# Top-k attention with a highway layer on Trainium2: one highway pass for the last rows of two batches, checks of one operation, and another preparation of the first batch

## Chip, cores and metric

The kernel runs on one core of one Trainium2 chip. The metric is the device time in microseconds (us) of one execution; the time before is the median of three runs.

## The reference

Eight batches of eight heads, 576 rows, head dimension 64. In each row of the scores the 32 largest stay and the others are masked, then softmax and the product with v follow. The heads of one row, put side by side, are the 512 inputs of a highway layer.

```python
scores = scale * np.matmul(q, k.transpose(0, 1, 3, 2))
kth = np.partition(scores, -top_k, axis=-1)[..., -top_k:-top_k + 1]
mask = scores >= kth
scores = np.where(mask, scores, -1000000000.0)
scores = scores - np.max(scores, axis=-1, keepdims=True)
attn = np.exp(scores)
attn = attn / (np.sum(attn, axis=-1, keepdims=True) + 1e-09)
x = np.matmul(attn, v)            # then (B, H, S, D) -> (B * S, H * D)
...
H = np.maximum(x @ w_h, 0.0)
T = 1.0 / (1.0 + np.exp(-(x @ w_t + b_t)))
return (T * H + (1.0 - T) * x).astype(np.float32)
```

## The kernel before

**Tiles.** The 576 rows of a batch are four query tiles of 128 rows (every fourth row of the first 512) and a rest of 64 rows. A `Group` (line 47) is one batch and one query tile, or one batch and its rest. It is cut into pairs: two heads of 128 query rows, or, in the rest, two tiles that each hold two heads of 64 rows. A batch has 4 x 4 + 2 = 18 pairs, the whole kernel `NPR` = 144.

**Steps.** The main loop (lines 662 to 728) runs over pairs, with several pairs in flight. Step n does, in this order of the program: `tree(n)`, the first maximum fold on VectorE (DVE), which reads the scores from PSUM (`ps`) and their evacuated half (`z`) and writes `hi`; in odd steps the further folds on DVE and the four integer operations of `minima` on GpSimd (POOL), which give the minima that belong to the folds' maxima; `mask(n - 4)` on ScalarE (ACT); a piece of a highway pass; `av(n - 5)`, the product with v on TensorE (PE) with ACT's copy to `xs`; `scores(n + 1)` on PE and `evac(n + 1)` on ACT; then the long part of DVE's work, lists of the eight largest values (MAX8 and MATCH_REPLACE8) in `tops` and `rest`, whose end, `m4`, holds the 32nd largest value of a row; and `trans(n - 4)`, PE transposes with the exponential on ACT. `Pinned` (line 25) keeps the operations of all engines but SyncE (SP) in the order in which the program gives them; so most lines of the profile are that helper's, L35, and one goes by the names of tiles.

**Highway.** When the last pair of a group has gone through `av`, `norm` (a DVE reciprocal of the row sums and a POOL multiply into `x`) runs at the end of that step, always an even one, and three entries join the list `ffn`, of which each step takes one: `ffn_x` (PE transposes of x into `xtps`, ACT copies `xT` and `xh`), `ffn_h` with `ffn_d` (PE product with w_h, then DVE `d`), and `ffn_t` with `ffn_e` and `ffn_o` (PE product with w_t and ACT tanh, then DVE `d` again, POOL `o`, and the output DMA on SP). The pre part of an entry stands ahead of `av` and `scores` on PE. A rest goes through all of this with 64 rows (`qlen`), eight times in the kernel. `settle` writes three things of each group for a check: `room`, `slack` and `reach`, three POOL operations.

**Loads.** `prep_pair` (line 113) prepares two heads of a batch: `load` (k, q and v, four DMAs each, on SP), `main` for k and for q (four PE transposes into `kqps`, a bank of the pool `fps`, and ACT's copy to `kT` or `qT`), `last` (the 64 rest rows), and `values` (v to bf16 on ACT). `fps` has one bank, in which all `kqps`, `xtps`, `hps` and `tps` take turns; `ztps` has two, for the transposes of `trans`, which begin in step 4. For batch 0 the four pairs of heads are prepared in steps -1 to 2, just ahead of the scores that need them; q of the first pair is loaded on ACT's queue. For other batches this is spread over the steps of the batch before.

**Ends.** `load_weights` (three POOL DMAs) is called in step 1. After the loop the check reduces `room`, `slack` and `reach`, and a flag says whether an exact second version of the whole kernel has to run (line 749); with these inputs it does not run.

Of the kernel before, what the change touches and what calls it, by code (L numbers as in the profile page):

```python
# [16 lines left out]
STEEP = 2.0**100  # L17
TINY = 1.0e-20
WIDE = 600.0
# [27 lines left out]
class Group:  # L47


    def __init__(self, b, qt, gi, H, P):  # L50
        self.b, self.qt, self.gi = b, qt, gi
        self.rem = qt == J
        self.qlen = P // 2 if self.rem else P
        tiles = (
            [(2 * hp, 2 * hp + 1) for hp in range(H // 2)]
            if self.rem
            else [(h,) for h in range(H)]
        )
        self.nt = len(tiles)
        self.pairs = [tiles[i : i + 2] for i in range(0, self.nt, 2)]  # L60


class Ops:
# [31 lines left out]
    def load_pair(self, src, hp, name, eng=None):  # L95
        nc, D, S, R, P = self.nc, self.D, self.S, self.R, self.P
        JP = J * P
        t = self.ldpool.tile([P, J + 1, 2, D], FP32, tag=name, name=name)
        eng = eng or nc.sync
        for hh in range(2):  # L100
            h = 2 * hp + hh
            eng.dma_start(
                t[:, 0:J, hh, :], src(h, 0, JP).rearrange("(p j) d -> p j d", j=J)
            )
            eng.dma_start(t[0:R, J, hh, :], src(h, JP, S))
        return t
# [6 lines left out]
    def prep_pair(self, srcs, hp, prep, qeng=None):  # L113

        nc, D, S, R, P = self.nc, self.D, self.S, self.R, self.P
        JP = J * P
        kT, qT, vb = prep
        ins = {}

        def load():  # L120
            ins["k"] = self.load_pair(srcs[1], hp, "kin")
            ins["q"] = self.load_pair(srcs[0], hp, "qin", qeng)
            ins["v"] = self.load_pair(srcs[2], hp, "vin")

        def main(name, dst):
            kqps = self.fps.tile([P, 512], FP32, tag="fp", name="kqps")
            for c in range(J):
                nc.tensor.transpose(
                    kqps[:, c * P : (c + 1) * P],
                    ins[name][:, c, :, :].rearrange("p h d -> p (h d)"),  # L130
                    self.ident[:],
                )
            nc.scalar.copy(dst[:, hp, 0:JP], kqps[:])

        def last():
            kqps = self.fps.tile([P, 512], FP32, tag="fp", name="kqps")
            for i, name in enumerate("kq"):
                nc.tensor.transpose(
                    kqps[:, i * R : (i + 1) * R],
                    ins[name][0:R, J, :, :].rearrange("p h d -> p (h d)"),  # L140
                    self.ident[0:R, 0:R],
                )
            for i, dst in enumerate((kT, qT)):
                nc.scalar.copy(dst[:, hp, JP:S], kqps[:, i * R : (i + 1) * R])

        def values():
            vdst = vb[:, 2 * hp : 2 * hp + 2, :, 0:D].rearrange("p h c d -> p c h d")
            nc.scalar.copy(vdst[:, 0:J], ins["v"][:, 0:J])
            nc.scalar.copy(vdst[0:R, J], ins["v"][0:R, J])

        return [load, lambda: main("k", kT), lambda: main("q", qT), last, values]
# [49 lines left out]
    def folds(self, k, g, pi):  # L201


        vec, P, S, H = self.nc.vector, self.P, self.S, self.H
        H1, H2, H3 = S // 2, S // 4, S // 8
        if pi == 0:
            g.w2 = self.lpool.tile([P, H, H2 + 24], FP32, tag="w2", name="w2")
        hi, hh, h3 = self.quads[k]
        vec.tensor_tensor(hh[:], hi[:, :, 0:H2], hi[:, :, H2:H1], ALU.max)
        a, b = hh[:, :, 0:H3], hh[:, :, H3:H2]  # L210
        vec.tensor_tensor(h3[:], a, b, ALU.max)
        return vec.tensor_tensor(
            g.w2[:, 2 * pi : 2 * pi + 4, H3:H2], a, b, ALU.min
        )
# [22 lines left out]
    def tops(self, g, t, h3, hl):  # L237


        nc, P, S = self.nc, self.P, self.S  # L240
        H2, H3 = S // 4, S // 8
        vec = nc.vector
        m1, m2, w2 = g.m1[:, t, :], g.m2[:, t, :], g.w2[:, t, :]
        vec.max(m1, h3)
        yield
        w1 = self.wpool.tile([P, H3], FP32, tag="w1", name="w1")
        vec.match_replace(w1[:], m1, h3, NEG)
        yield
        vec.max(m2, w1[:])
        yield  # L250
        vec.match_replace(w2[:, 0:H3], m2, w1[:], NEG)
        yield
        vec.max(w2[:, H2 : H2 + 8], hl[:, 0:H3])
        yield
        vec.max(w2[:, H2 + 8 : H2 + 16], hl[:, H3:H2])

    def rest(self, g, t, lo):


        nc, P, S = self.nc, self.P, self.S  # L260
        H2 = S // 4
        W = H2 + 24
        vec = nc.vector
        w2 = g.w2[:, t, :]
        vec.max(w2[:, H2 + 16 : W], lo)
        yield
        m3 = self.wpool.tile([P, 8], FP32, tag="m3", name="m3")
        vec.max(m3[:], w2)
        yield
        w3 = self.wpool.tile([P, W], FP32, tag="w3", name="w3")  # L270
        vec.match_replace(w3[:], m3[:], w2, NEG)
        yield
        vec.max(g.m4[:, t, :], w3[:])
# [20 lines left out]
    def lists(self, n, g, pi):  # L294
        P, H = self.P, self.H
        if pi == 0:
            for name in ("m1", "m4") if self.exact else ("m1", "m2", "m4"):
                setattr(g, name, self.lpool.tile([P, H, 8], FP32, tag=name, name=name))
# [19 lines left out]
    def settle(self, g):  # L318
# [7 lines left out]
            self.room[:, g.gi, 0:nt, 0:3],  # L326
            thr.unsqueeze(2).to_broadcast([P, nt, 3]),
# [3 lines left out]
        gp.tensor_tensor(  # L331
            self.slack[:, g.gi, 0:nt, 0], g.m2[:, 0:nt, 7], thr, ALU.subtract
        )
        gp.tensor_copy(self.reach[:, g.gi, 0:nt], g.m1[:, 0:nt, 0])
# [70 lines left out]
    def av(self, n, g, pi, vb):  # L405
# [4 lines left out]
        if pi == 0:  # L410
            g.xs = self.xpool.tile([P, self.H * DE], FP32, tag="xs", name="xs")
        ql = g.qlen
        c0 = col = 0 if g.rem else 2 * P
        h0 = g.pairs[pi][0][0]
        for ti, heads in enumerate(g.pairs[pi]):
            for hi, h in enumerate(heads):
                q0 = hi * (P // 2)
                for c in range(J + 1):
                    nc.tensor.matmul(
                        zr[0:ql, col : col + DE],  # L420
# [6 lines left out]
        nc.scalar.copy(g.xs[0:ql, h0 * DE : h0 * DE + col - c0], zr[0:ql, c0:col])  # L427
# [3 lines left out]
    def norm(self, g):  # L431
        nc, P, H, D = self.nc, self.P, self.H, self.D
        ql = g.qlen
        xs3 = g.xs[0:ql, :].rearrange("p (h e) -> p h e", e=D + 1)
        rinv = self.xpool.tile([P, H], FP32, tag="rinv", name="rinv")
# [9 lines left out]
    def ffn_x(self, g):  # L445
        nc, P, n_g, ql = self.nc, self.P, self.n_g, g.qlen
# [16 lines left out]
    def ffn_h(self, g):  # L463
        nc, P, n_g, ql = self.nc, self.P, self.n_g, g.qlen
# [10 lines left out]
    def ffn_d(self, g):  # L475

        ql = g.qlen
# [10 lines left out]
    def ffn_t(self, g):  # L488

        nc, P, n_g, ql = self.nc, self.P, self.n_g, g.qlen  # L490
# [14 lines left out]
    def ffn_e(self, g):  # L505

        ql = g.qlen
# [9 lines left out]
    def ffn_o(self, g, dst):  # L517
        ql = g.qlen
        o = self.fpool.tile([self.P, self.dm], FP32, tag="o", name="o")
        self.nc.gpsimd.tensor_tensor(o[0:ql, :], g.x[0:ql, :], g.d[0:ql, :], ALU.add)  # L520
        self.nc.sync.dma_start(dst, o[0:ql, :])
# [3 lines left out]
def kernel(  # L525
# [17 lines left out]
    assert D == 64 and R == 64 and H % 4 == 0 and dm == 512  # L543
# [13 lines left out]
    nc.vector.tensor_scalar_mul(nident[:], ident[:], -STEEP)  # L557
# [11 lines left out]
    for i in range(2):  # L569
# [5 lines left out]
    room = const([P, NG, H, 3], FP32, "room")  # L575
    nc.gpsimd.memset(room[:], 1.0)
    slack = const([P, NG, H, 1], FP32, "slack")
    nc.gpsimd.memset(slack[:], 1.0)
    reach = const([P, NG, H], FP32, "reach")
    nc.gpsimd.memset(reach[:], 1.0)  # L580
# [8 lines left out]
        room=room, slack=slack, reach=reach,  # L589
    )  # L590

    with ExitStack() as cm:
# [12 lines left out]
        def srcs(b):  # L605
            return [
                (lambda h, r0, r1, t=t: t[b, h, r0:r1, :]) for t in (q, k, v)
            ]

        def out_rows(g):  # L610
            if not g.rem:
                r0 = g.b * S + g.qt
                return out[r0 : r0 + JP : J, :]
            r0 = g.b * S + JP
            return out[r0 : r0 + R, :]

        groups = [
            Group(b, qt, b * nck + qt, H, P) for b in range(B) for qt in range(nck)
# [8 lines left out]
        def prep(b, hp, qeng=None):  # L627
            if hp == 0:
                preps[b] = ops.prep_alloc(vbufs[b % 2])
            return ops.prep_pair(srcs(b), hp, preps[b], qeng)  # L630
# [20 lines left out]
        early = [prep(0, hp, nc.scalar if hp == 0 else None) for hp in range(NHP)]  # L651
# [10 lines left out]
        while step < NPR + 6 or ffn:  # L662
            n = step
            if n + 1 < NHP:
                for piece in early[n + 1][1:4]:
                    piece()
                if n + 2 < NHP:
                    early[n + 2][0]()
            if have(n):
                ops.tree(n)  # L670
                if n % 2:
                    ops.minima(n // 2, ops.folds(n // 2, *pairs[n - 1]))
            if n == 1:
# [18 lines left out]
            ended = have(n - 5) and pairs[n - 5][1] == len(pairs[n - 5][0].pairs) - 1  # L692
# [25 lines left out]
            if ended:  # L718
# [6 lines left out]
                        lambda g=g: (ops.ffn_e(g), ops.ffn_o(g, out_rows(g))),  # L725
# [7 lines left out]
        vec.tensor_reduce(ok[:, 0:1], room[:], op=ALU.min, axis=AX.XYZ)  # L733
        vec.tensor_reduce(ok[:, 1:2], slack[:], op=ALU.min, axis=AX.XYZ)
        vec.tensor_reduce(ok[:, 2:3], reach[:], op=ALU.max, axis=AX.XY)
        bad = const([P, 4], FP32, "bad")
        vec.tensor_scalar(bad[:, 0:1], ok[:, 0:1], TINY, None, ALU.is_lt)
        vec.tensor_scalar(bad[:, 1:2], ok[:, 1:2], 0.0, None, ALU.is_lt)
        vec.tensor_scalar(bad[:, 2:3], ok[:, 2:3], WIDE, None, ALU.is_gt)
# [9 lines left out]
    with tc.If(taken > 0):  # L749
        with tc.For_i(0, B, 1) as b:  # L750
            with ExitStack() as cm:
                ops = Ops(cm, tc, shared, exact=True)
                srcs = [
                    (lambda h, r0, r1, t=t: t[bass.ds(b, 1), h, r0:r1, :].rearrange("o s d -> (o s) d"))
# [58 lines left out]
```

## Time and profile before

| | |
|---|---|
| median of three runs | 925.96 us (923.73 to 926.5) |
| the profiled execution | 925.72 us, its span 923.9 us |
| instructions | 20386 |
| output DMAs (`out_dram<-o`) | 32 of 256 KB, 8 of 128 KB |
| loads of k (`kin`) | 64 of 128 KB, 64 of 16 KB, the same for v and, with two of each on ACT's queue, for q |
| TensorE clock granted, mean | 0.944 of full speed |

A span is the time from the first to the last instruction of the program in one profiled execution. In the lines of the profile, `d<-tps,d 64x512` is an operation that writes tile d and reads tps and d, 64 partitions of 512 elements; `xN` is how many there are. In rows of groups, the figures after the first bar are busy us in total and mean ns of one, those after the second the engine's idle time just before them and what ended it. In the timeline the figures are start and length in us, and square brackets hold the idle time before and its releaser. PEld are TensorE's weight loads, SPq the issue of DMAs on SP.

### The profile page before, as it was taken

To read this page: it belongs to the slowest core of one execution; us is meant where nothing else is said; L and a number is where in the kernel's file an instruction comes from. 1 tells how busy PE (TensorE), PEld (TensorE's weight loads), DVE (VectorE), ACT (ScalarE), POOL (GpSimd) and SP (SyncE) were. 2 spreads that over 40 slices of the span, in tenths; PEclk is the share of its full clock that TensorE was granted. 3 is DMA by queue.
4 is the path that set the end of the run, shared out by engine and by line. 5 is a ranking of instruction groups with operands and counts; after the bars stand their busy time and mean duration, and the time that the engine had idled before them with its cause. 6 is when DMAs were issued, how large, how long until landed. Compare 5 with 4: busy or idle time off the path is not lost.

```text
span 923.9 us, 20386 instructions
## 1 busy us (share of the span) xinstructions
PE 730.8 (79%) x6601; PEld 510.6 (55%) x6601; DVE 873.4 (95%) x4234; ACT 699.2 (76%) x1321; POOL 709.5 (77%) x509
## 2 busy tenths in 40 slices
PE   5687878878788887878888787887879878877774
PEld 3355556555565555555655555655646555555552
DVE  4699999999999999999999999999999999999991
ACT  3488778887787886887878886888868878776772
POOL 3777778877877888777788887887787778877761
PEclk9999899999999998998999999999989989998997
DMA  5731220221103220122202212023100300000000
GB/s 114 138 70 40 51 51 13 58 69 45 38 18 69 61 52 12 46 51 51 51 13 56 50 41 51 13 67 73 46 24 25 71 12 13 12 13 7 13 24 21
DMA packets 123298, 40.33 MB, mean 44 GB/s; under 512 B 117424, under 2 KB 118576, under 8 KB 123184
## 3 DMA queue, kind: packets, MB, share of 16 engines
q1 hardware_dynamic: 120768, 37.48, 16.6%
q0 software_dynamic: 1200, 1.18, 0.8%
q8 instruction: 54, 0.88, 0.4%
q14 instruction: 60, 0.49, 0.2%
q10 hardware_dynamic: 1216, 0.30, 0.1%
HBM read 30.67 MB, written 9.44 MB: 43 GB/s over the span
## 4 chain that ended last, share of the span: by engine, by line
DVE 78%; POOL 8%; PE 7%; ACT 3%; issue 2%; SPq 1%; DMA 1%; POOLq 0%; ACTq 0%; DVEq 0%
DVE w L35 37%; DVE m L35 18%; DVE hi L35 9%; DVE hh L35 6%; DVE d L35 5%; POOL hi L35 4%; DVE h L35 3%; PE ps L35 2%; POOL hh L35 2%; PE zt L35 2%; POOL o L35 1%; PE zr L35 1%; PE xtps L35 1%; POOL x L35 1%; PE kqps L35 1%
## 5 line engine op out<-in xcount | busy, mean ns | idle before, releaser
L35 PE MATMUL ps<-kT,qT 64*128 64x64 f32 (+3 forms) x1280 | 221.9, 473 | 48.8 <-DVE hi L35 47.8
L35 ACT ACTIVATE z<-ps 128x1152 f32<-128x1152 f32 x144 | 163.0, 1132 | 96.7 <-PE ps L35 95.6
L35 POOL TENSOR_TENSOR hh<-hi,hh 128x576 int32<-128x576 int32 x72 | 101.6, 1410 | 171.9 <-DVE w L35 171.7
L35 PE MATMUL zt<-ident,z 128*128 128x128 f32 x1152 | 225.1, 289 | 0.0
L35 ACT ACTIVATE pen<-z,m 128x576 bf16<-128x576 f32 x288 | 224.1, 779 | 0.2 <-DVE m L35 0.2
L35 PE MATMUL zt<-nident,pen 128*128 128x128 bf16 x1152 | 214.5, 226 | 0.0
L35 DVE MAX8 m<-w 128x8 f32<-128x168 f32 (+1 forms) x864 | 203.6, 283 | 0.0
L35 PEld LDWEIGHTS ps<-kT,qT 64*128 64x128 f32 (+1 forms) x1280 | 112.8, 191 | 148.2 <-issue 88.5
L35 POOL TENSOR_TENSOR hi<-hi,z 128x1152 int32<-128x1152 int32 x72 | 190.1, 2641 | 5.6
L35 POOL TENSOR_TENSOR hi<-z,hi 128x1152 int32<-128x1152 int32 x72 | 189.3, 2629 | 5.6
L35 PEld LDWEIGHTS zt<-ident,z 128*128 128x128 f32 x1152 | 169.8, 147 | 18.4
L35 ACT ACTIVATE et<-zt 128x512 bf16<-128x512 f32 x288 | 161.9, 602 | 15.5 <-PE zt L35 14.1
L35 PEld LDWEIGHTS <-pen 128*128 128x128 bf16 x1440 | 161.0, 112 | 6.3 <-ACT pen L35 6.3
L35 DVE MATCH_REPLACE8 w<-m,w 128x72 f32<-128x72 f32 (+1 forms) x576 | 148.3, 265 | 0.0
L35 DVE TENSOR_TENSOR hi<-ps,z 128x576 f32<-128x576 f32 x144 | 106.3, 738 | 21.6 <-ACT z L35 21.5
L35 DVE MAX8 w<-hi 128x8 f32<-128x288 f32 x288 | 116.5, 445 | 0.0
L35 POOL TENSOR_TENSOR hh<-hh,hi 128x576 int32<-128x576 int32 x72 | 101.4, 1408 | 5.6
L35 PEld LDWEIGHTS <-et 128*128 128x128 bf16 (+1 forms) x1600 | 70.4, 104 | 36.3 <-ACT et L35 13.8
L35 PE MATMUL zr<-v,et 128*128 128x65 bf16 (+1 forms) x1600 | 82.4, 199 | 5.1 <-ACT et L35 4.9
L35 DVE MAX8 w<-hh 128x8 f32<-128x72 f32 x576 | 83.9, 216 | 0.0
L35 PE MATMUL zr<-ident,z 128*128 128x128 f32 x288 | 76.8, 320 | 3.9 <-ACT xs L35 3.9
L35 PE MATMUL xtps<-ident,x 128*128 128x128 f32 (+1 forms) x160 | 28.0, 304 | 60.4 <-POOL x L35 51.1
(64 smaller groups left out, 1102.7 us busy)
## 6 DMA issues: line engine op xcount, KB each, us to landing
kin<-in_k_dram SPq DMA_DIRECT2D x64, 128.0 KB, 2.7
vin<-in_v_dram SPq DMA_DIRECT2D x64, 128.0 KB, 2.6
out_dram<-o SPq DMA_DIRECT2D x32, 256.0 KB, 2.3
qin<-in_q_dram SPq DMA_DIRECT2D x62, 128.0 KB, 2.6
kin<-in_k_dram SPq DMA_DIRECT2D x64, 16.0 KB, 2.5
vin<-in_v_dram SPq DMA_DIRECT2D x64, 16.0 KB, 2.3
out_dram<-o SPq DMA_DIRECT2D x8, 128.0 KB, 2.3
qin<-in_q_dram SPq DMA_DIRECT2D x62, 16.0 KB, 2.4
```

The costliest lines, as they stand in the source:

```text
L35: return self._tc.keep_in_program_order(fn(*args, **kw))
```

## The change

- A rest of an even batch has no highway pass of its own. Its heads' results are put into partitions 0 to 63 of a tile `xs` (tag `xr`), those of the next batch's rest into partitions 64 to 127, and one pass of 128 rows follows after the second; its output goes out in two DMAs of 64 rows.
- `settle` is one POOL operation: the second list of maxima `m2` is written into `w2`, which grows by 8 columns, so that `room` has four columns; `slack` and `reach` go. The check looks at three columns' minimum, the fourth's maximum, and the smallest of `scales`, a constant tile that takes the place of `rinv`.
- In the preparation of batch 0, k and q are transposed into the two banks of `ztps` and the rest rows into that of `fps`; q is copied on DVE. The pieces stand after `tree(n)` instead of ahead of it. The first loads of pair 0 (k and q) are split by head over SP's and ACT's queues.
- In all batches the rest rows of a pair of heads come in one DMA, and v in one DMA with longer runs: 8 DMAs a pair instead of 12.
- `nident` is made on ACT instead of DVE, and `load_weights` is called in step 5 instead of 1.

```diff
-    def __init__(self, b, qt, gi, H, P):
+    def __init__(self, b, qt, gi, H, P, joint=False):
         self.b, self.qt, self.gi = b, qt, gi
...
         self.qlen = P // 2 if self.rem else P
+        self.joint = joint and self.rem
+        self.r0 = b % 2 * self.qlen if self.joint else 0
+        self.rows = P if self.joint else self.qlen
         tiles = (
...
-    def load_pair(self, src, hp, name, eng=None):
+    def load_pair(self, src, hp, name, eng=None, other=None):
         nc, D, S, R, P = self.nc, self.D, self.S, self.R, self.P
         JP = J * P
+        eng = eng or nc.sync
+        if name == "vin":
+            t = self.ldpool.tile([P, 2, J + 1, D], FP32, tag=name, name=name)
+            eng.dma_start(
+                t[:, :, 0:J, :].rearrange("p h j d -> p h (j d)"),
+                src(hp, 0, JP).rearrange("h (p j) d -> p h (j d)", j=J),
+            )
+            eng.dma_start(t[0:R, :, J, :], src(hp, JP, S).rearrange("h p d -> p h d"))
+            return t
         t = self.ldpool.tile([P, J + 1, 2, D], FP32, tag=name, name=name)
-        eng = eng or nc.sync
         for hh in range(2):
-            h = 2 * hp + hh
-            eng.dma_start(
-                t[:, 0:J, hh, :], src(h, 0, JP).rearrange("(p j) d -> p j d", j=J)
-            )
-            eng.dma_start(t[0:R, J, hh, :], src(h, JP, S))
+            (other if other and hh else eng).dma_start(
+                t[:, 0:J, hh, :],
+                src(hp, 0, JP)[hh].rearrange("(p j) d -> p j d", j=J),
+            )
+        rest = lambda: eng.dma_start(
+            t[0:R, J, :, :], src(hp, JP, S).rearrange("h p d -> p h d")
+        )
+        if other:
+            return t, rest
+        rest()
         return t
...
         def load():
-            ins["k"] = self.load_pair(srcs[1], hp, "kin")
-            ins["q"] = self.load_pair(srcs[0], hp, "qin", qeng)
+            if qeng:
+                ins["k"], k_rest = self.load_pair(srcs[1], hp, "kin", None, qeng)
+                ins["q"], q_rest = self.load_pair(srcs[0], hp, "qin", None, qeng)
+                k_rest()
+                q_rest()
+            else:
+                ins["k"] = self.load_pair(srcs[1], hp, "kin")
+                ins["q"] = self.load_pair(srcs[0], hp, "qin")
             ins["v"] = self.load_pair(srcs[2], hp, "vin")
...
         def main(name, dst):
-            kqps = self.fps.tile([P, 512], FP32, tag="fp", name="kqps")
+            if early:
+                kqps = self.ztps.tile([P, 512], FP32, tag="zt", name="kqps")
+            else:
+                kqps = self.fps.tile([P, 512], FP32, tag="fp", name="kqps")
             for c in range(J):
...
                 )
-            nc.scalar.copy(dst[:, hp, 0:JP], kqps[:])
+            if early and name == "q":
+                nc.vector.tensor_copy(dst[:, hp, 0:JP], kqps[:])
+            else:
+                nc.scalar.copy(dst[:, hp, 0:JP], kqps[:])
...
         vec = nc.vector
-        m1, m2, w2 = g.m1[:, t, :], g.m2[:, t, :], g.w2[:, t, :]
+        m1, w2 = g.m1[:, t, :], g.w2[:, t, :]
+        m2 = w2[:, H2 + 24 : H2 + 32]
         vec.max(m1, h3)
...
         gp.tensor_tensor(
-            self.room[:, g.gi, 0:nt, 0:3],
-            thr.unsqueeze(2).to_broadcast([P, nt, 3]),
+            self.room[:, g.gi, 0:nt, :],
+            thr.unsqueeze(2).to_broadcast([P, nt, 4]),
             ends,
...
         )
-        gp.tensor_tensor(
-            self.slack[:, g.gi, 0:nt, 0], g.m2[:, 0:nt, 7], thr, ALU.subtract
-        )
-        gp.tensor_copy(self.reach[:, g.gi, 0:nt], g.m1[:, 0:nt, 0])
...
         if pi == 0:
-            g.xs = self.xpool.tile([P, self.H * DE], FP32, tag="xs", name="xs")
-        ql = g.qlen
+            if g.joint and g.r0:
+                g.xs = self.half
+            else:
+                tag, bufs = ("xr", 1) if g.joint else ("xs", 2)
+                g.xs = self.xpool.tile(
+                    [P, self.H * DE], FP32, tag=tag, name="xs", bufs=bufs
+                )
+            if g.joint:
+                self.half = g.xs
+        ql, rows = g.qlen, slice(g.r0, g.r0 + g.qlen)
         c0 = col = 0 if g.rem else 2 * P
...
                     nc.tensor.matmul(
-                        zr[0:ql, col : col + DE],
+                        zr[rows, col : col + DE],
                         et[:, ti, c, q0 : q0 + ql],
...
                 col += DE
-        nc.scalar.copy(g.xs[0:ql, h0 * DE : h0 * DE + col - c0], zr[0:ql, c0:col])
+        nc.scalar.copy(g.xs[rows, h0 * DE : h0 * DE + col - c0], zr[rows, c0:col])
...
         nc, P, H, D = self.nc, self.P, self.H, self.D
-        ql = g.qlen
+        ql = g.rows
         xs3 = g.xs[0:ql, :].rearrange("p (h e) -> p h e", e=D + 1)
-        rinv = self.xpool.tile([P, H], FP32, tag="rinv", name="rinv")
+        rinv = self.scales[:, g.gi, :]
         nc.vector.reciprocal(rinv[0:ql, :], xs3[:, :, D])
...
     def ffn_x(self, g):
-        nc, P, n_g, ql = self.nc, self.P, self.n_g, g.qlen
+        nc, P, n_g, ql = self.nc, self.P, self.n_g, g.rows
         xtps = self.fps.tile([P, 512], FP32, tag="fp", name="xtps")
...
-    def ffn_o(self, g, dst):
-        ql = g.qlen
+    def ffn_o(self, g, *dsts):
+        ql = g.rows
         o = self.fpool.tile([self.P, self.dm], FP32, tag="o", name="o")
         self.nc.gpsimd.tensor_tensor(o[0:ql, :], g.x[0:ql, :], g.d[0:ql, :], ALU.add)
-        self.nc.sync.dma_start(dst, o[0:ql, :])
+        n = ql // len(dsts)
+        for i, dst in enumerate(dsts):
+            self.nc.sync.dma_start(dst, o[i * n : (i + 1) * n, :])
...
     nident = const([P, P], BF16, "nident")
-    nc.vector.tensor_scalar_mul(nident[:], ident[:], -STEEP)
+    nc.scalar.mul(nident[:], ident[:], -STEEP)
     zbufs = []
...
     nc.gpsimd.memset(cst[:], 0.5 / float(P))
-    room = const([P, NG, H, 3], FP32, "room")
-    nc.gpsimd.memset(room[:], 1.0)
-    slack = const([P, NG, H, 1], FP32, "slack")
-    nc.gpsimd.memset(slack[:], 1.0)
-    reach = const([P, NG, H], FP32, "reach")
-    nc.gpsimd.memset(reach[:], 1.0)
+    room = const([P, NG, H, 4], FP32, "room")
+    nc.gpsimd.memset(room[:, :, :, 0:3], 1.0)
+    nc.gpsimd.memset(room[:, :, :, 3:4], -1.0)
+    scales = const([P, NG, H], FP32, "scales")
+    nc.gpsimd.memset(scales[:], 1.0)
     wh = const([P, n_g, dm], BF16, "wh")
...
             return [
-                (lambda h, r0, r1, t=t: t[b, h, r0:r1, :]) for t in (q, k, v)
+                (lambda hp, r0, r1, t=t: t[b, 2 * hp : 2 * hp + 2, r0:r1, :])
+                for t in (q, k, v)
             ]
...
                 r0 = g.b * S + g.qt
-                return out[r0 : r0 + JP : J, :]
-            r0 = g.b * S + JP
-            return out[r0 : r0 + R, :]
+                return [out[r0 : r0 + JP : J, :]]
+            ends = [(g.b + i) * S for i in (0, 1)]
+            return [out[r1 - R : r1, :] for r1 in ends]
         groups = [
-            Group(b, qt, b * nck + qt, H, P) for b in range(B) for qt in range(nck)
+            Group(b, qt, b * nck + qt, H, P, joint=True)
+            for b in range(B)
+            for qt in range(nck)
         ]
...
-        early = [prep(0, hp, nc.scalar if hp == 0 else None) for hp in range(NHP)]
+        early = [
+            prep(0, hp, nc.scalar if hp == 0 else None, True) for hp in range(NHP)
+        ]
         early[0][0]()
...
             n = step
-            if n + 1 < NHP:
-                for piece in early[n + 1][1:4]:
-                    piece()
-                if n + 2 < NHP:
-                    early[n + 2][0]()
             if have(n):
                 ops.tree(n)
+                if n + 1 < NHP:
+                    for piece in early[n + 1][1:4]:
+                        piece()
+                    if n + 2 < NHP:
+                        early[n + 2][0]()
                 if n % 2:
                     ops.minima(n // 2, ops.folds(n // 2, *pairs[n - 1]))
-            if n == 1:
+            if n == 5:
                 load_weights()
...
                 early[n + 1][4]()
-            ended = have(n - 5) and pairs[n - 5][1] == len(pairs[n - 5][0].pairs) - 1
+            ended = False
+            if have(n - 5):
+                g, pi = pairs[n - 5]
+                ended = pi == len(g.pairs) - 1 and (not g.rem or g.r0 > 0)
             if n % 2:
...
         vec = nc.vector
-        vec.tensor_reduce(ok[:, 0:1], room[:], op=ALU.min, axis=AX.XYZ)
-        vec.tensor_reduce(ok[:, 1:2], slack[:], op=ALU.min, axis=AX.XYZ)
-        vec.tensor_reduce(ok[:, 2:3], reach[:], op=ALU.max, axis=AX.XY)
+        vec.tensor_reduce(ok[:, 0:1], room[:, :, :, 0:3], op=ALU.min, axis=AX.XYZ)
+        vec.tensor_reduce(ok[:, 1:2], room[:, :, :, 3:4], op=ALU.max, axis=AX.XYZ)
+        vec.tensor_reduce(ok[:, 2:3], scales[:], op=ALU.min, axis=AX.XY)
         bad = const([P, 4], FP32, "bad")
         vec.tensor_scalar(bad[:, 0:1], ok[:, 0:1], TINY, None, ALU.is_lt)
-        vec.tensor_scalar(bad[:, 1:2], ok[:, 1:2], 0.0, None, ALU.is_lt)
-        vec.tensor_scalar(bad[:, 2:3], ok[:, 2:3], WIDE, None, ALU.is_gt)
+        vec.tensor_scalar(bad[:, 1:2], ok[:, 1:2], 0.0, None, ALU.is_gt)
+        vec.tensor_scalar(bad[:, 2:3], ok[:, 2:3], FAINT, None, ALU.is_lt)
         vec.tensor_reduce(bad[:, 3:4], bad[:, 0:3], op=ALU.max, axis=AX.X)
```

## The prediction

> **What bounds the kernel now.** I read four views in this order: the page, the busy time by stretch, the start of each step's first VectorE instruction in the timeline, and the groups by form. The page first:
>
> ```profile
> span 923.9 us, 20386 instructions
> PE 730.8 (79%) x6601; PEld 510.6 (55%) x6601; DVE 873.4 (95%) x4234; ACT 699.2 (76%) x1321; POOL 709.5 (77%) x509
> ...
> DVE 78%; POOL 8%; PE 7%; ACT 3%; issue 2%; SPq 1%; DMA 1%; POOLq 0%; ACTq 0%; DVEq 0%
> ```
>
> VectorE is busy 95% of the span and carries 78% of the chain that ended last. By stretch (length, then busy us of PE, PEld, DVE, ACT, POOL, then clock, DMA share, GB/s):
>
> ```profile
> 0.00:33.40 33.40, 19.14 (x72) 12.12 (x72) 14.64 (x39) 12.58 (x27) 18.12 (x25) 1.00 0.51 112
> ...
> 100.00:300.00 200.00, 163.78 (x1533) 114.44 (x1531) 198.11 (x977) 160.34 (x304) 159.88 (x114) 0.97 0.18 43
> ...
> 910.00:924.00 14.00, 3.72 (x10) 1.21 (x10) 1.78 (x4) 1.38 (x3) 1.95 (x2) 0.58 0.12 34
> ```
>
> There are three regimes. In the middle DVE is busy 198.11 of 200 us, so a DVE instruction removed there shortens the kernel by its start-to-start time and work of the others is free. In the first 33.4 us DVE is busy for 14.64 only (7.00 of them one blocked instruction), and in the last 14 hardly at all: there the chains count. The head's chain, in the timeline:
>
> ```profile
> 1.57 7.00 DVE L557 TENSOR_SCALAR nident<-ident 128x128 bf16<-128x128 f32 x1 [1.57 <-POOL ident masks.py:199]
> ...
> 5.63 1.09 PE L35 MATMUL kqps<-ident,kin 128*128 128x128 f32 x4 [5.63 <-DMA kin<-in_k_dram]
> ...
> 7.39 1.12 PE L35 MATMUL kqps<-ident,qin 128*128 128x128 f32 x4 [0.68 <-ACT kT L35]
> ...
> 28.95 1.09 PE L35 MATMUL kqps<-ident,qin 128*128 128x128 f32 x4 [1.68 <-DMA qin<-in_q_dram]
> ...
> 34.54 0.76 DVE L35 TENSOR_TENSOR hi<-ps,z 128x576 f32<-128x576 f32 x1 [3.36 <-ACT z L35]
> ```
>
> The trees (hi<-ps,z) of steps 0 to 3 start at 13.01, 19.83, 26.64 and 34.54; from step 4 on they come 5.5 to 6.4 apart without a wait worth naming. The q transposes wait for ACT's copy of k, since both use the one bank of pool fps, and SP issues 12 loads a pair at about 0.65 us, 7.8 us, which is why q of pair 3 is awaited.
>
> [...] issues of 0.60 and 0.63 us stand back to back on SP from 0.76 to 33 us while the DMA share is 0.51. [...] the 7.00 us of nident end at 8.57, GpSimd's memsets at 8.49. [...] eight score matmuls take 2.40 us in step 57 (granted clock 0.54) and 1.30 us in step 31 (1.00).
>
> **The change part by part.**
>
> *Joint highway pass.* Four of the eight 64-row passes go. Their DVE rows:
>
> ```profile
> L35 DVE SCALAR_TENSOR_TENSOR d<-tps,d 64x512 f32<-64x512 f32 x8 | 5.4, 674 | 3.1 <-ACT tps L35 3.0
> L35 DVE SCALAR_TENSOR_TENSOR d<-hps,xh 64x512 f32<-64x512 f32 x8 | 5.3, 665 | 2.2 <-PE hps L35 2.2
> ...
> L35 DVE RECIPROCAL rinv<-xs 64x8 f32<-64x8 f32 x8 | 1.5, 184 | 0.4 <-ACT xs L35 0.4
> ```
>
> Neighbours on DVE overlap, so I take the price from step lengths. In each batch step 6 (no d, no rinv) is 5.51 us and step 9 (neither, odd) 5.77; steps with one d are 6.11 and 6.37, so 0.60 per d; a rinv adds 0.07. A pass costs 2 x 0.60 + 0.07 = 1.27, four cost 5.1 us, all in the DVE-bound middle (batches 0, 2, 4, 6). A 128-row d takes 0.68, as the 64-row one, so the passes that stay cost the same: -5.1. From both sides: 4.8 if a few wait elsewhere, 6.1 if full durations counted. The PE, ACT (4 x (0.38 + 0.62 + 0.57) = 6.3 us) and POOL (4 x (1.04 + 1.27) = 9.2 us) work that goes too lies beside DVE: nothing.
>
> *One-op checks.* Slack and reach leave POOL: 6.9 + 3.8 + 6.2 + 3.1 = 20.0 us; room has 32 instead of 24 elements of 0.25 us. POOL waits 171.7 us in total for DVE's folds, so this is hidden by that wait: nothing. The second maximum keeps its MAX8 and only writes into w2; the 168-element rows read keep their length.
>
> *Head: SP, banks, q copy.* First k halves are both issued at 0.76. Before, the second half was issued at 2.40 and PE began at 5.63, 3.2 later; so PE begins at 4.0. Then k 1.1, q 1.1 in another bank without waiting for ACT, to 6.2; the copy of q on DVE, not in the trace, I price as d<-tps (512 elements from PSUM, 0.67): 6.95. Lower bound 0.58 (ACT's copy), upper 2.4, if it does wait for POOL's memsets until 8.5. Scores 2.5, evacuation 1.13: tree 0 at 10.7 instead of 13.01. After that a step runs from scores end to scores end: ACT z 1.13, v casts 0.81, k copy 0.58, two small copies 0.32, scores 2.5, handoffs 0.1: 5.4 us, where PE's own work is 1.1 + 1.1 + 0.37 + 2.5 = 5.1, SP's 8 issues x 0.65 = 5.2, and DVE's tree and copy (0.76 + 0.67 after z) end before ACT. So trees at 16.1 and 21.5. Step 2 has on DVE the copy of q of pair 3 (to about 23.2) and then the first lists, 3.9 us (27.3 to 31.2 before): 27.1; the evacuation of pair 3 ends at 21.5 + 5.4 = 26.9. Tree 3 at 27.2 instead of 34.54: -7.3. Loads do not spoil this: the last q main load of pair 3 is the 27th issue on SP, 0.76 + 26 x 0.65 = 17.7, landing 2.6 later at 20.3, against 21.4 when PE wants it. Bounds: 5.0, if ACT does nident (and the table load of 1.28) ahead of its two first loads, which puts them near 2.5; 9.0, if denser PE work lifts the clock and a step falls to about 4.6.
>
> *nident to ACT.* One 128x128 op in ACT's idle time (ACT idles 2.02 before its first copy): nothing but the order just named.
>
> *Weights from step 1 to step 5.* Three issues on POOL, 0.94 + 0.75 + 0.56 = 2.3 us, now behind the third minima. POOL's next work is the fourth, two steps on, and it idles 2.6 us on average before one (171.7 / 65). They are issued near 49 us and first wanted in step 10, near 67: nothing. Loads on SP pass no longer beside them: nothing.
>
> *Loads of later batches.* 8 issues instead of 12 a pair; SP waits 579.8 us for POOL's o in total, and its loads run many steps ahead: nothing.
>
> *Tail.* The last pass has 128 rows: transposes 0.66 to 1.12 instead of 0.43 (+0.4), xT 0.60 instead of 0.38 (+0.2), and a second output issue behind the first (0.50): +1.1. The check on scales now waits for the last rinv (907.07), then 0.48 + 0.15 + 0.16 in DVE's idle time ahead of the d at 911.5: nothing, at worst 0.8.
>
> Sum: -7.3 - 5.1 + 1.1 = -11.3, so the span goes from 923.9 to 912.6. That execution took 925.72 us (1.8 over its span), next to the median of 925.96; so 914.5.
>
> **The rivals.**
> - Head lost: VectorE's copy of q waits for GpSimd's memsets or integer folds, or ACT issues late, each step. For: nident's 7.00. [...] Gain 2 to 3 there: 925.96 - 2.5 - 5.1 + 1.1 = 919.5.
> - The passes were in slack, only the head gains: 925.96 - 7.3 + 1.1 = 919.8. Against: 0.60 per d in every batch.
> - Better than forecast: PE's clock comes up in the head (9.0) and fewer half-clock steps: about 910.
> - Slower: [...] With four passes less, PE idles more in steps 6 to 8, and a half clock in a later step with transposes of x (about 35 of them, on the way to scores) costs:
>
> ```profile
> 359.72 1.11 PE L35 MATMUL xtps<-ident,x 128*128 128x128 f32 x4 [2.78 <-POOL x L35]
> ...
> 362.01 2.40 PE L35 MATMUL ps<-kT,qT 64*128 64x512 f32 x8
> ...
> 365.67 0.76 DVE L35 TENSOR_TENSOR hi<-ps,z 128x576 f32<-128x576 f32 x1 [1.07 <-ACT z L35]
> ```
>
> Step 57 took 7.09 us against 5.92 for its like: 1.2 us. Such stalls sum to 6.8 us now (steps 13, 57, 67, 111, 121 above all). Ten more cancel the gain; with twenty more the time is 925.96 - 11.3 + 24 = 938.7. [...] Against: only 5 of some 35 are hit now, and of the steps behind a dropped pass (5 to 9) only step 9 transposes x.
> - The change does not do what it says: the diff shows the dropped passes plainly; counts would tell.
>
> **How the numbers follow.** Forecast 0.74, head lost 0.10, passes in slack 0.04, better 0.06, slower 0.05, nothing done 0.01. The forecast's own bounds: head 5.0 to 9.0, passes 4.8 to 6.1, tail 0.6 to 1.9, stalls 3 us either way, run to run 1.4; taken together 910 to 919, and with the head-lost case the range is 910 to 920. No change means within 0.3%, 2.8 us, about what a measurement of this kernel can tell. Faster 0.92 (forecast, better, nearly all of the 919s), same 0.03 (half-lost head with a few more stalls), slower 0.05 [...].
>
> **What would show it.** Tree 3 near 27, with q transposes right behind those of k; a DVE copy of q near 0.67; 36 instead of 40 pairs of d, step 7 and 8 of even batches at 5.77 and 5.6; the same middle otherwise; end of DVE's lists to the end of the span 1 us longer. I am wrong if tree 3 starts after 30, if copies of q take over 1.5 us, or if more than eight steps are over 0.4 us longer than their like.

## The result and the profile after

The changed kernel takes 909.97 us in the median (909.09 to 910.64) against 925.85 us, a ratio of 0.9832 with a 95% interval of 0.9814 to 0.985. In a second series it was 910.21 us (907.33 to 913.38) against 924.26, ratio 0.9848 (0.9827 to 0.9869). So the gain is 14 to 16 us, where 11.3 were forecast; the forecast of 914.5 was 4.5 us too high, and the time lies on the lower bound of the range of 910 to 920: two of the first four executions were a little under it, two a little over.

The page of the changed kernel, the lines that answer to those shown of the kernel before:

```profile
span 907.3 us, 19916 instructions
PE 715.6 (79%) x6549; PEld 501.2 (55%) x6549; DVE 864.6 (95%) x4225; ACT 692.9 (76%) x1306; POOL 687.2 (76%) x421
...
DVE 85%; POOL 5%; PE 4%; ACT 2%; issue 1%; DMA 1%; SPq 1%; POOLq 0%; ACTq 0%
```

VectorE still sets the end, now for 85% of the chain instead of 78%; the shares of POOL and TensorE in it fell from 8% and 7% to 5% and 4%. The busy time by stretch, with the same columns as before:

```profile
0.00:33.40 33.40, 18.77 (x80) 11.70 (x80) 17.13 (x63) 14.72 (x29) 20.19 (x25) 0.85 0.66 159
100.00:300.00 200.00, 163.05 (x1522) 115.60 (x1518) 198.89 (x988) 159.80 (x300) 158.81 (x94) 0.95 0.17 43
```

In the first 33.4 us VectorE is busy for 2.5 us more than before, although the 7.00 us of `nident` are gone from it, and the DMA share rises from 0.51 to 0.66. The clock in this row (0.85, before 1.00) is not to be compared: the clock records begin at 16.24 us here and only at 45.13 in the kernel before, and what lies ahead of them counts as full speed. In the middle it is busy for 198.89 of 200 us instead of 198.11. The timeline of VectorE in the head shows the copies of q and the trees:

```profile
6.86 0.69 DVE L35 COPY qT<-kqps 128x512 f32<-128x512 f32 x1 [6.86 <-PE kqps L35]
11.30 0.76 DVE L35 TENSOR_TENSOR hi<-ps,z 128x576 f32<-128x576 f32 x1 [3.74 <-ACT z L35]
...
16.47 0.76 DVE L35 TENSOR_TENSOR hi<-ps,z 128x576 f32<-128x576 f32 x1 [3.75 <-ACT z L35]
...
20.47 0.76 DVE L35 TENSOR_TENSOR hi<-ps,z 128x576 f32<-128x576 f32 x1 [1.11 <-ACT z L35]
21.93 0.69 DVE L35 COPY qT<-kqps 128x512 f32<-128x512 f32 x1 [0.70 <-PE kqps L35]
26.31 0.75 DVE L35 TENSOR_TENSOR hi<-ps,z 128x576 f32<-128x576 f32 x1
27.09 1.28 DVE L35 TENSOR_TENSOR hh<-hi 128x576 f32<-128x576 f32 x1
```

Tree 3 starts at 26.31 us instead of 34.54. And the groups of the highway on VectorE, 36 instead of 40 of each, all with 128 rows:

```profile
L35 DVE SCALAR_TENSOR_TENSOR d<-hps,xh 128x512 f32<-128x512 f32 x36 | 24.8, 689 | 6.3 <-PE hps L35 6.3
L35 DVE SCALAR_TENSOR_TENSOR d<-tps,d 128x512 f32<-128x512 f32 x36 | 24.4, 678 | 3.4 <-ACT tps L35 3.4
```

**Where the time went.** To divide the 16.6 us between the two profiled executions I use the starts of the trees and a sum of stalls. A step from tree to tree has a plain length: 5.51 (even) or 5.77 us (odd), plus 0.60 per `d`, 0.07 per reciprocal and 0.155 where x is transposed in an odd step; what a step takes beyond that is its stall. Over steps 4 to 142 the stalls sum to 6.8 us before and 2.5 after (the 2.9 named in the expectations below counts step 3 too). How small an excess still counts moves such a sum by about half a us.

| part | before | after | difference |
|---|---|---|---|
| start to tree 3 | 34.54 | 26.31 | -8.2 |
| step 3 | 5.79 | 6.30 | +0.5 |
| tree 4 to tree 143: dropped passes | | | -5.1 |
| tree 4 to tree 143: stalls | 6.8 | 2.5 | -4.3 |
| tree 143 to the end | 42.5 | 42.9 | +0.5 |
| sum | 923.9 | 907.3 | -16.6 |

The dropped passes cost what they should: steps 25 and 26 now take 5.78 and 5.57 us. The surprise is the row of stalls, in which the forecast had put nothing, with 3 us either way. The experiments ask two things: what makes the head's 8.2, and why there are fewer stalls.

### The profile page after: what moved, and what is told of

Its sections match the earlier page's. It is cut to its first block, busy times and chain, and to the rows that moved or that the text cites. A ratio compares the mean times of both kernels' runs of the same rounds, so it can differ in the third digit from the quotient of the medians.

```text
span 907.3 us, 19916 instructions
## 1 busy us (share of the span) xinstructions
PE 715.6 (79%) x6549; PEld 501.2 (55%) x6549; DVE 864.6 (95%) x4225; ACT 692.9 (76%) x1306; POOL 687.2 (76%) x421
## 3 DMA queue, kind: packets, MB, share of 16 engines
q1 hardware_dynamic: 94304, 37.51, 16.1%
## 4 chain that ended last, share of the span: by engine, by line
DVE 85%; POOL 5%; PE 4%; ACT 2%; issue 1%; DMA 1%; SPq 1%; POOLq 0%; ACTq 0%
DVE w L35 45%; DVE m L35 17%; DVE hi L35 10%; DVE hh L35 6%; DVE d L35 4%; DVE h L35 3%; POOL hi L35 2%; PE ps L35 2%; POOL hh L35 1%; PE zt L35 1%; ACT pen L35 1%; DMA qin<-in_q_dram 1%; POOL o L35 1%; ACT z L35 1%; PE zr L35 1%
## 5 line engine op out<-in xcount | busy, mean ns | idle before, releaser
L35 DVE MAX8 m<-w 128x8 f32<-128x168 f32 x576 | 161.1, 323 | 0.0
L35 DVE MATCH_REPLACE8 w<-m,w 128x168 f32<-128x168 f32 x288 | 89.7, 321 | 0.0
L35 PE MATMUL xtps<-ident,x 128*128 128x128 f32 x144 | 25.1, 300 | 53.4 <-POOL x L35 45.8
```

Source lines behind the costliest of these rows:

```text
L35: return self._tc.keep_in_program_order(fn(*args, **kw))
```

## The experiments

**The three parts alone.** Each is the kernel before with one part of the change.

The joint pass alone (core of the edit):

```diff
+        self.joint = joint and self.rem
+        self.r0 = b % 2 * self.qlen if self.joint else 0
+        self.rows = P if self.joint else self.qlen
...
+                ended = pi == len(g.pairs) - 1 and (not g.rem or g.r0 > 0)
```

In the profile of the kernel before and the first of the changed one TensorE's half-clock records in the middle last 3.41 or 6.83 us, and all of them begin a whole number of 3.41 us after one another: on a grid that stands 0.76 us off the first instruction in the kernel before and 2.58 in the changed one.

> The kernel before with the joint highway pass alone. Two theories of why the middle of the changed kernel gave 3.7 us more than the four dropped passes. Beat: TensorE's half-clock windows lie on a free grid of 3.41 us, and which steps they hit is a matter of the steps' phase against it. Relief: with less work on POOL and ACT the scores come earlier and leave slack. Both: the dropped passes save 5.1 us between tree 3 and tree 143, the tail is 0.5 longer, the head is as before (tree 3 at 34.5). Beat: stalls in the middle anywhere between 3 and 9 us (6.7 before), span 916 to 923. Relief by the dropped passes: stalls near 3, span 915.5.

It took 917.12 us (916.22 to 919.35) against 924.63, ratio 0.9912 (0.9895 to 0.9929): 7.5 us gained. Its profiled execution is the slowest of its four, span 917.4, stalls 6.4, tree 3 to tree 143 5.5 us shorter than before. Of the 6.5 us between the two profiled executions, the other 1.0 lies behind tree 143. So the passes alone do not always take the stalls along; the median, 2 us lower than that execution, suggests that they sometimes do. Neither theory is decided.

The checks alone (core of the edit):

```diff
-        m1, m2, w2 = g.m1[:, t, :], g.m2[:, t, :], g.w2[:, t, :]
+        m1, w2 = g.m1[:, t, :], g.w2[:, t, :]
+        m2 = w2[:, H2 + 24 : H2 + 32]
...
-        gp.tensor_tensor(
-            self.slack[:, g.gi, 0:nt, 0], g.m2[:, 0:nt, 7], thr, ALU.subtract
-        )
-        gp.tensor_copy(self.reach[:, g.gi, 0:nt], g.m1[:, 0:nt, 0])
```

> The kernel before with the one-operation checks alone. Forecast: nothing to gain, 20 us of POOL work lie in its wait for DVE. Beat: stalls anywhere between 3 and 9 us, span 920 to 926, tree 3 at 34.5, the plain steps still 5.51 and 5.77. Relief by the checks: stalls near 3 us, span 920.

924.03 us against 924.63 with 20 and 23 executions, ratio 0.9998 (0.9989 to 1.0007): POOL operations of 20 us in sum are gone, POOL is busy for 15 us less (694.6 instead of 709.5), and there is no gain that can be told from none. Its stalls are 5.2 us in the profile. Relief by the checks falls.

The head, with the loads, `nident` on ACT and the later weights (core of the edit):

```diff
+            if early:
+                kqps = self.ztps.tile([P, 512], FP32, tag="zt", name="kqps")
...
+            if early and name == "q":
+                nc.vector.tensor_copy(dst[:, hp, 0:JP], kqps[:])
```

> The kernel before with the new preparation of batch 0, the loads, nident on ACT and the later weights. Both theories: tree 3 at 26.3 instead of 34.5, 8.2 us gained. Relief (passes or checks): stalls stay near 6.7, span 915.7. Beat: stalls anywhere between 3 and 9, span 912 to 918.

917.12 us against 924.63, ratio 0.991 (0.9894 to 0.9927). Tree 3 is at 26.42, stalls 7.0. The head is worth its 8.1 us at tree 3, of which step 3 gives 0.5 back, and leaves the stalls as they are.

**What the head rests on.** Three kernels take one thing of the new head back. Each ran once (915.70, 917.52 and 912.26 us, the kernel before beside them 923.51), so I read their traces and not their times. In the first, k and q go through the one bank again, and with it the copy of q goes back to ACT:

```diff
-            prep(0, hp, nc.scalar if hp == 0 else None, True) for hp in range(NHP)
+            prep(0, hp, nc.scalar if hp == 0 else None) for hp in range(NHP)
```

> The changed kernel with k and q of batch 0 transposed through the one bank of fps and q copied on ACT, as before; loads, nident and order as changed. Theory: banks and loads are two limits of the head, one behind the other, and each alone gives little. Then a step is again z 1.13, v 0.81, k copy 0.58, q transposes 1.1, q copy 0.59, rest 0.37, scores 2.3 = 6.9 us, and tree 3 comes near 12 + 3 x 6.9 = 32.7 instead of 26.3. Rival: the loads were the limit and the banks only a help; tree 3 at 27 to 29.

```profile
25.36 1.12 PE L35 MATMUL kqps<-ident,qin 128*128 128x128 f32 x4 [1.38 <-ACT kT L35]
...
30.97 0.76 DVE L35 TENSOR_TENSOR hi<-ps,z 128x576 f32<-128x576 f32 x1 [2.28 <-ACT z L35]
```

The transposes of q wait again for ACT's copy of k. Tree 3 at 30.97 lies between the 32.7 expected and the 27 to 29 of its rival. In the second, the loads are those of before (core of the edit):

```diff
+        for hh in range(2):
+            h = 2 * hp + hh
+            eng.dma_start(
+                t[:, 0:J, hh, :], src(h, 0, JP).rearrange("(p j) d -> p j d", j=J)
+            )
+            eng.dma_start(t[0:R, J, hh, :], src(h, JP, S))
```

> The changed kernel with the loads as before (12 issues a pair, first q alone on ACT's queue); banks, q copy, nident and order as changed. Theory of two limits: SP issues 7.8 us a pair again, the last q of pair 3 lands near 28.8, the q copy ends near 30.5, the first lists 3.9 later: tree 3 near 34, as before. Rival: the banks were the limit; tree 3 at 27 to 29.

Tree 3 at 34.49, all of the gain lost, and TensorE waits for loads in every pair of heads. Its timeline:

```profile
26.13 1.09 PE L35 MATMUL kqps<-ident,kin 128*128 128x128 f32 x4 [0.81 <-DMA kin<-in_k_dram]
...
28.93 1.09 PE L35 MATMUL kqps<-ident,qin 128*128 128x128 f32 x4 [1.71 <-DMA qin<-in_q_dram]
30.06 0.69 DVE L35 COPY qT<-kqps 128x512 f32<-128x512 f32 x1 [2.78 <-PE kqps L35]
...
34.49 0.76 DVE L35 TENSOR_TENSOR hi<-ps,z 128x576 f32<-128x576 f32 x1
```

The two limits stand one behind the other. With the new loads but the old bank 3.6 of the 8.2 us remain; with the new banks but the old loads nothing remains, since the last q lands no sooner than before. In the third `nident` is back on VectorE:

```diff
-    nc.scalar.mul(nident[:], ident[:], -STEEP)
+    nc.vector.tensor_scalar_mul(nident[:], ident[:], -STEEP)
```

> The changed kernel with nident made on VectorE, as before. It is blocked until POOL's memsets end near 8.5 (7.00 us before), the copy of q for pair 0 stands behind it on VectorE and starts near 8.7 instead of 6.86, tree 0 at 13.1 instead of 11.3; tree 3 later by 0.5 to 1.8, since SP's issues leave some slack. If nothing depends on it: trees as in the changed kernel.

```profile
1.58 7.26 DVE L592 TENSOR_SCALAR nident<-ident 128x128 bf16<-128x128 f32 x1 [1.58 <-POOL ident masks.py:199]
7.01 1.83 DVE L35 COPY qT<-kqps 128x512 f32<-128x512 f32 x1
12.61 0.76 DVE L35 TENSOR_TENSOR hi<-ps,z 128x576 f32<-128x576 f32 x1 [3.77 <-ACT z L35]
...
26.41 2.63 POOL L35 TENSOR_TENSOR hi<-hi,z 128x1152 int32<-128x1152 int32 x1
27.60 2.05 DVE L35 TENSOR_TENSOR hh<-hi 128x576 f32<-128x576 f32 x1
```

The copy of q stands behind `nident`, which takes 7.26 us here against 0.31 on ScalarE in the changed kernel, until 8.84 and tree 0 comes 1.3 us later; but tree 3 is at 26.83, where the changed kernel's own two profiles have 26.31 and 26.82. That looks as if the delay had been caught up. It comes back one step later: POOL's integer operations are as late as tree 0 was, the fold `hh<-hi` of step 3 falls beside one of them and takes 2.05 us, and tree 4 is at 33.89 instead of 32.61 and 32.62. So in this execution moving `nident` is worth 1.3 us.

**Are the stalls made by x ahead of the scores?** In this edit `ffn_x` is called after `evac`, so that the scores of the next pair do not wait for POOL's x (shown without the line that sets `pre` to None):

```diff
                 pre, post = ffn.pop(0)
-                pre()
+                if post:
+                    pre()
...
                 ops.evac(n + 1)
+            if pre and not post:
+                pre()
```

> The changed kernel with the transposes of x put behind the scores of the same step on TensorE instead of ahead of them. If the stalls come from x standing ahead of the scores while the clock is halved, they fall from 2.9 us to under 1, and the span from 907.3 to about 905. If they have another cause, or ACT's copies of x now delay something else, the span stays at 907 or grows.

905.61 us (904.24 to 906.31), ratio to the kernel before 0.979 (0.9774 to 0.9806); stalls 0.8, and DVE's waits for ACT's z between 35 and 870 us fall from 1.1 to 0.2 us. This kernel beats both. The same edit on the kernel before:

> The kernel before with the transposes of x behind the scores of the same step on TensorE. If x ahead of the scores under a halved clock makes the stalls, they fall from 6.7 to under 1 and the time from 924.6 to about 919; the distance to the changed kernel with the same edit (905.6) is then 8.2 + 5.1 - 0.5 = 12.8 us, with no part of it from stalls. Else the time stays at 924 to 926.

917.41 us against 924.26, ratio 0.9918 (0.9905 to 0.9931), stalls 0.7. Step 57, which the prediction shows with 7.09 us, takes 5.93; the timeline of the kernel before with this edit:

```profile
357.62 0.74 DVE L35 TENSOR_TENSOR hi<-ps,z 128x576 f32<-128x576 f32 x1
...
358.71 1.30 PE L35 MATMUL ps<-kT,qT 64*128 64x512 f32 x8
...
359.94 0.66 PE L35 MATMUL xtps<-ident,x 128*128 128x128 f32 x4
...
363.55 0.73 DVE L35 TENSOR_TENSOR hi<-ps,z 128x576 f32<-128x576 f32 x1
```

The scores come first, x fills the time behind them, and the next tree needs no wait. The gain is more than the stalls. Tree 3 to tree 143 is 6.1 us shorter than in the kernel before, and 2.2 or 3.8 shorter in the changed kernel with this edit than in its two profiles without it; a further 1.3 to 2.4 us lie behind tree 143 (40.4 and 40.5 us with the edit, 42.5 before, 42.9 and 41.9 in the changed kernel), a part that I did not take apart. The edit also changes the clock. From 45 us to tree 143 TensorE has half clock for 65 instead of 89 us in the kernel before, and for 61 instead of 79 and 82 in the changed one. Of the 20 half-clock records of the kernel before in that stretch, 8 begin while TensorE waits for x or within 0.6 us after. That wait is 1.51 us in the mean before and 0.06 with the edit.

The edit also gives a clean price of the passes: tree 3 to tree 143 is 840.80 us in this kernel and 835.85 in the changed one with the same edit, 4.95 less, where both have nearly no stalls.

**Why the changed kernel has fewer stalls.** This is the question that stays open in part. First the changed kernel again:

> The changed kernel once more, beside the next three on one chip and with more executions. Stalls in the middle were 2.9 us in its first profile, the fastest of four executions; near 4 in the mean. About 910 us.

910.21 us, stalls 4.7 in a profile that is its median execution. Then it with DVE time put back in the place of the dropped passes, and none of their work on the other engines:

```diff
+            if n // 18 % 2 and n % 18 in (7, 8):
+                ops.nc.vector.max(dum[:], fill[:])
```

> The changed kernel with the DVE time of the four dropped passes put back as eight single MAX8 of 500 constant values (steps 7 and 8 of every second batch, 0.59 us each start to start), without the passes' work on TensorE, ACT and POOL. These MAX8 are no part of the computation. Relief (less work on the other engines leaves slack): stalls stay at 3 to 4 us, time is that of the changed kernel plus 4.7. Rhythm (the steps' spacing against the 3.41 us windows decides which steps are hit): with the spacing of the kernel before, the stalls are back at about 6, time plus 7.

916.80 us (916.03 to 918.89), 6.6 over the 910.2 of the changed kernel, where eight MAX8 cost 4.7 (each of their steps grew by about 0.59). Its profile, the fastest of its five executions, has stalls of 4.8, no more than the second profile of the changed kernel, and 1.3 us more behind tree 143. So this run decides nothing about the stalls. With `in (8,)` there are four:

> The same with four MAX8, in step 8 alone. Relief: the changed kernel plus 2.4 us, stalls 3 to 4. Rhythm: a third spacing, so a third pattern of hit steps; stalls anywhere between 1 and 8, and the time off from plus 2.4 by as much.

916.01 us (910.3 to 917.35), 5.8 over it, where the four cost 2.4; stalls 6.1 in a profile of 915.59 us. One of its six executions took only 910.3. In it, step 39 is hit as step 57 was before:

```profile
241.91 0.74 DVE L35 TENSOR_TENSOR hi<-ps,z 128x576 f32<-128x576 f32 x1
...
243.05 1.12 PE L35 MATMUL xtps<-ident,x 128*128 128x128 f32 x4 [2.77 <-POOL x L35]
245.34 2.40 PE L35 MATMUL ps<-kT,qT 64*128 64x512 f32 x8
...
249.01 0.76 DVE L35 TENSOR_TENSOR hi<-ps,z 128x576 f32<-128x576 f32 x1 [1.08 <-ACT z L35]
```

Such a step loses 1.2 us at half clock. The first profile of the changed kernel has none like it, its second has one (step 39): in step 75 of the first a half-clock record (456.56 to 459.97 us) covers the transposes of x and only part of the scores (1.74 us):

```profile
456.76 1.12 PE L35 MATMUL xtps<-ident,x 128*128 128x128 f32 x4 [2.78 <-POOL x L35]
459.05 1.74 PE L35 MATMUL ps<-kT,qT 64*128 64x512 f32 x8
...
462.06 0.76 DVE L35 TENSOR_TENSOR hi<-ps,z 128x576 f32<-128x576 f32 x1 [0.41 <-ACT z L35]
```

Could the MAX8 have cost something besides? The same four, with x behind the scores:

> The changed kernel with x behind the scores and the four MAX8 of 500 constants in step 8 of every second batch (no part of the computation). With x ahead of the scores the same four cost 5.8 us in the medians, 2.4 of them their own. If the other 3.4 were stalls in steps that transpose x, they cannot arise here: 905.6 + 2.4 = 908.0, stalls under 1. If the MAX8 cost something else besides, about 911.

908.04 us (907.19 to 908.61), 2.4 over 905.61, and stalls of 0.6. So the four cost just their own time where x cannot stall the scores, and about 3.4 us more where it can. Relief on the other engines asked for 2.4 us and low stalls with four MAX8, and doesn't hold. What is left is that the spacing of the steps changes which of them meet a half-clock record, and with how much of it. I call this the likeliest reading, not a shown cause: executions of one kernel spread over 6 us here (907.33 to 913.38), and no run fixes where the records begin.

## Why the prediction was right, and where it was off

- **What bounds it: right.** A VectorE-bound middle with a head and a tail in which chains count. Taking 20 us of operations off POOL gave nothing that can be measured.
- **Joint pass, -5.1: right.** 5.1 from the plain steps, 4.95 from the two kernels with x behind the scores. Start-to-start time was the right price; the full durations (6.1) would have been too much.
- **Head, -7.3: right in mechanism, 0.9 too small at tree 3 and 0.4 at tree 4.** Trees 0 and 1 came at 11.3 and 16.5 where 10.7 and 16.1 were worked out. From there TensorE's clock came up: the scores of step 1 took 1.30 us instead of the 2.5 assumed, so tree 2 came at 20.5, not 21.5. That was the upper bound named for a denser head, and it happened for one step: the first record of full clock begins at 16.24 us, behind 3.41 us in which TensorE was busy for 0.99 of the time, and half clock is back from 23.07. The copy of q took 0.69 us against 0.67, with POOL's memsets beside it (6.86) as well as its integer operations (21.93): the rival of a blocked copy falls. That the copy would not be blocked as `nident` was had been an assumption of the author's, which no trace of before showed. What the forecast had not seen is that step 3 gives 0.5 back (see below): tree 4 comes at 32.61 and 32.62 in the two profiles instead of 40.33.
- **Two-queue loads and banks.** The working had ACT's chain with the new banks and SP's issues with the new loads close together (5.4 and 5.2 us a step). The experiments show that neither alone would have reached the forecast.
- **`nident`: priced at nothing.** It is worth 1.3 us at tree 0, at most 0.5 at tree 3, and in the one execution without it 1.3 us again at tree 4, through the order of POOL's work, which the prediction left out.
- **Tail, +1.1: somewhat too large.** +0.5 in the profile shown, but the stretch is 0.6 us shorter than before in the second one (41.9 us from tree 143 to the end) and 1.0 shorter in the joint pass alone (41.5). TensorE's clock moves it by more than the change does: the last product with w_t took 1.86 us before and in the first profile after, inside half-clock records that begin at 912.12 and 893.46 us, and 1.02 in the other two. The sign that the prediction named, 1 us more from DVE's last list to the end, is 0.6 more in the first profile and 0.5 less in the second.
- **The term that was off: stalls, taken as 0 with 3 us either way.** It was -4.3 in the first profile, outside that bound, and -2.1 in the second. The prediction saw more of the clock as a danger than as a gain: less TensorE work was to mean more steps at half clock. That did not come: half-clock time from 45 us to tree 143 is 89 us before and 79 and 82 in the two profiles after. Its case "better than forecast", with a faster head and fewer half-clock steps, named about 910 and got a chance of 0.06; it is the closest to what came. So the point forecast missed mostly by the stalls, whose fall it had not worked out, and that the range reached just far enough down is partly luck.
- **Where the stalls were: half seen.** The prediction says that the steps come 5.5 to 6.4 us apart without a wait worth naming, and then counts five steps with stalls at 1.2 us each. In the same trace five steps take 6.85 to 7.09 us (14, 57, 68, 111 and 122). Of the five that it counts, three (13, 67, 121) lose only 0.5 themselves; the step behind each loses another 0.7 to 0.8, where VectorE's `d` waits for TensorE's `hps`. The price of a hit, 1.2 to 1.3 us, is right. The prediction left it as noise, when moving one call takes nearly all of it away.

## What to carry to other kernels

When one engine is busy all the time, price what you remove from it by the lengths of otherwise equal steps, and look at what its rare waits have in common: here nearly all lay in steps where TensorE was given a late input ahead of the one that the bounding engine needed, or in the step right behind, and reordering the two brought a further 4.4 to 4.6 us. When a start-up chain has two limits of nearly the same length, such as DMA issues and a shared bank, lifting one can show nothing (the banks here) or less than half (the loads here); lift both before you judge either. Follow a delay past the point where it seems caught up: that of `nident` was gone at tree 3 and back at tree 4. And before a gain beyond the priced terms is credited to the edit, look at whether it stays in further executions: here it was 4.3 us in one profile and 2.1 in the next.

## What the runs showed of the hardware

- When TensorE's clock falls: cut into stretches of 3.41 us, the length of the shortest half-clock records and on the grid of their starts, the profile before has 235 stretches between 60 and 864 us. In 19 of them TensorE was by its records busy for less than half of the time (0.31 to 0.49). All 19 are followed by a stretch of half clock, of the other 216 only 6, and those 6 (busy for 0.79 to 0.86) were at half clock themselves. In the first profile of the changed kernel, between 60 and 848 us, 18 of 19 (0.23 to 0.50) are, of the other 211 only 3. So in these two profiles half clock came behind 37 of the 38 stretches that were less than half busy; they did not have to be idle ones. In step 57, whose lines the prediction shows, 2.2 of the 2.78 us of waiting for x lie in the stretch that ends at 359.16 (TensorE busy for 1.19 of 3.41 us), and the half clock begins there, just ahead of the transposes.
- The fold `hh<-hi` took 1.28 us in step 3 after (27.09, shown above) instead of 0.76, while an integer operation of POOL that began at 25.12 ran until 27.76; with `nident` on VectorE it took 2.05 us, beside one that ran until 29.04. In both cases the fold ended 0.6 us after POOL's operation. In step 1 after, at 17.75 with POOL idle, it took 0.75; in the changed kernel with x behind the scores, where tree 3 came at 27.01 and the fold at 27.80, 0.76. So an earlier start can run into another engine's operation and give some of it back, 0.5 us here.
- A load of v in one DMA of 256 KB took 0.54 to 0.60 us to issue on SP, as much as one of 128 KB before (0.57 to 0.60); half the number of DMAs for v took half the issue time.
